# Weight conversion between attention and the first MLP: sign bit on GpSimd, value in PSUM, one piece every second period

## The chip, the cores and the metric

The kernel runs on one core of one Trainium2 chip. The metric is the device time of one execution in microseconds (us), lower is better. Engines are named as in the profile: PE is TensorE (PEld its weight loads), DVE is VectorE, ACT is ScalarE, POOL is GpSimd, SP is SyncE, whose queue starts nearly all of the DMA transfers.

## The reference

Attention over 4 batches, 8 heads, 576 positions and head dimension 64, with a learned bias that depends on relative position; then two MLPs on the 2304 tokens, each 512 to 2048 to 512:

```python
scores = scale * q @ k.T + bias            # bias = relu(x @ w1 + b1) @ w2, x from log1p of |i - j|
attn = softmax(scores);  x = attn @ v      # 2304 x 512 after the heads are put side by side
h = x @ w_in;   g = h - tanh(h);           x = g @ w_out       # first MLP
h = x @ w_in2;  r = max(h, 0); g = s*r*r + b;  out = g @ w_out2  # second MLP
```

The four weight matrices reach the kernel as 64-bit floats. The MLPs multiply in a split form: each operand becomes a rounded part ("high", fp32r) and the rest ("low"), and a product is three matmuls (high x high, high x low, low x high).

## The kernel before, in words

**Stages.** First the position bias is computed and written to DRAM. Then attention runs as 80 *periods*: 16 head pairs, `t` = 0 to 4 in each, two heads of 128 query rows per period (at `t` = 4, one tile of the two 64-row rests). Five periods are one pair. Then the MLPs run as 10 chunks of tokens (five of each layer; 512 tokens, one chunk of each layer 256), each with 16 *iterations* over the hidden blocks `f`.

**Order.** The order on every engine is the order in which the program is written (manual schedule); each engine works its own queue in that order and waits by semaphores. In iteration `n` of the attention loop the code emits: the normalisation of period n-2 (`emit_norm`, POOL, tile `pn`), the scores of period n (`emit_score`, PE, tile `s` in PSUM, two buffers), exp and row sum of n-1 (ACT; the sum `sm` gets an epsilon on POOL), bias and row minimum of n (`emit_bias`, DVE, L389, tiles `raw` and `mn`), the reciprocal of n-1 (DVE), transposes of n-3 (PE, L426) and their copies out of PSUM to `pt` (ACT and DVE), the products with V (PE, L481). At the end of the iteration come loads, pieces of the first chunk's input for the MLP (list `XPRE`: a load of `x`, its rounding "hi", L84, and rest "lo", L87, both on POOL), and weight conversion.

**Weight conversion.** A *half* is one 128 x 512 block of `w_in` or `w_out`; 32 halves make a layer. `wq` lists them in the order of use, `fetch` loads them. The two 32-bit words of each 64-bit number are turned into one fp32 value by integer arithmetic. One call of `weights_tick` is a pipeline of three halves:

- for half a: ACT scales the high word into tile `wx` (L138); DVE cuts out the sign bit into tile `wsg` (L139);
- for half a-1: DVE shifts the value and ors the sign in (L130), then ors in the top bits of the low word (L142);
- for half a-2: ACT rounds to the high part (L122), POOL subtracts to get the low part (L87).

In attention `TK` places 16 such calls (every fourth period from 15, then 66, 70, 74, 78). In the MLP loop, iteration n makes calls until `want` halves are done: 14 at the start, then 1.65 per iteration from n = 3; for the second layer's weights 1.4 per iteration from the fifth chunk on.

**MLP iteration.** `gemm1` (PE, 12 matmuls into the PSUM tile `h`, four buffers), `gate` (ACT reads `h` into `t`; DVE computes g into SBUF from `h` and `t`, in layer 2 from `t` alone and with a second instruction), then one iteration later `split` (ACT rounds g to `gh`, DVE subtracts to get `gl`), and two iterations later `gemm2` (12 matmuls into four PSUM accumulators).

Of the kernel before, what the change touches and what calls it, by code (L numbers as in the profile page):

```python
# [10 lines left out]
F32 = mybir.dt.float32  # L11
# [18 lines left out]
NW0 = 7  # L30

# [15 lines left out]
TK = [*range(15, 63, 4), 66, 70, 74, 78]  # L47
# [11 lines left out]
def tile_kernel(ctx, tc, qk, vd, wcat, wts, sb, ltab, psib, ipsi8, out):  # L59
# [26 lines left out]
    def rest(lo, raw, hi):  # L86
        nc.gpsimd.tensor_tensor(out=lo, in0=raw, in1=hi.bitcast(F32), op=ALU.subtract)  # L87
# [25 lines left out]

    def weights_tick():

        a, b_, c = wdone
        if c < b_:
            F, h = wq[c]
            x = wx_t.pop(c)[0]
            wdone[2] += 1  # L120
            w = wt[F, h] = slot(F, h, [2, 512], F32R)
            nc.scalar.copy(w[:, 0], x)  # L122
            rest(w[:, 1], x, w[:, 0])
        half = b_ < a
        if half:

            wdone[1] += 1
            x, sg = wx_t[b_]
            xi = x.bitcast(I32)
            nc.vector.scalar_tensor_tensor(out=xi, in0=xi, scalar=3, in1=sg,  # L130
                                           op0=ALU.logical_shift_left, op1=ALU.bitwise_or)
        if a < len(wq) and wq[a] in raw_w:

            wdone[0] += 1
            y = wst.tile([128, 512], F32, tag="wx", name="wx")
            sg = wsg.tile([128, 512], I32, tag="wsg", name="wsg")
            hw = raw_w[wq[a]][:, :, 1]
            nc.scalar.activation(out=y, in_=hw.bitcast(F32), func=AF.Copy, scale=2.0 ** -112)  # L138
            nc.vector.tensor_scalar(out=sg, in0=hw, scalar1=-2 ** 31, scalar2=1, op0=ALU.bitwise_and, op1=ALU.bitwise_or)  # L139
            wx_t[a] = (y, sg)  # L140
# [133 lines left out]
    def ring(dtype):  # L274
        return bp.tile([128, S], dtype, tag="bias", name="ring")
# [40 lines left out]
    def gate(c, f):  # L316
        layer, _, cn = CHUNKS[c]
        h = h_t.pop((c, f))
        g = ring(F32)[:, 0:cn]
        t = ring(F32)[:, 0:cn]  # L320
        if layer == 0:
            nc.scalar.activation(out=t, in_=h, func=AF.Tanh)  # L322
            nc.vector.tensor_tensor(out=g, in0=h, in1=t, op=ALU.subtract)  # L323
        else:
            nc.scalar.activation(out=t, in_=h, func=AF.Relu)  # L325
            nc.vector.tensor_tensor(out=g, in0=t, in1=t, op=ALU.mult)  # L326
            nc.vector.tensor_scalar(out=g, in0=g, scalar1=sb_t[:, 0:1], scalar2=sb_t[:, 1:2], op0=ALU.mult, op1=ALU.add)  # L327
        g_t[c, f] = (g, ring(F32R)[:, 0:cn], ring(F32R)[:, 0:cn])
# [7 lines left out]
    with ExitStack() as ca:  # L336
# [23 lines left out]
        TICKS = {n: TK.count(n) for n in TK}  # L360
# [140 lines left out]
        for n in range(NK + 6):  # L501
# [29 lines left out]
            for _ in range(TICKS.get(n, 0)):  # L531
                weights_tick()
# [7 lines left out]
    with ExitStack() as cb:  # L540
# [46 lines left out]
        xwork = {}  # L587
        seq = [(c, f) for c in range(len(CHUNKS)) for f in range(NF)]
# [4 lines left out]
        for n in range(len(seq) + LAG):  # L593
            want = min(32, 2 * NW0 + max(0, int(1.65 * (n - 3))))
# [85 lines left out]
```

## Time and profile before

| | |
|---|---|
| median of 3 runs | 1091.99 us (1091.46 to 1092.54) |
| the profiled execution: its own time, its span | 1091.09 us, 1089.3 us |
| PE busy | 1065.3 us (98%) |
| DVE busy | 642.6 us (59%) |
| ACT busy | 469.6 us (43%) |
| POOL busy | 327.5 us (30%) |
| attention, roughly | 48 to 303 us of the span |
| both MLPs | 303 to 1085 us of the span |

A matmul's end is modelled, so a busy PE need not be at its peak: what an engine waited for is read from idle time and its releaser, and from how far apart the same step of successive periods starts. PE's granted clock is at its upper level (2.4 GHz) in all but a few us of the span.

### The profile page before, as it was taken

To read this page: it belongs to the slowest core of one execution; us is meant where nothing else is said; L and a number is where in the kernel's file an instruction comes from. 1 tells how busy PE (TensorE), PEld (TensorE's weight loads), DVE (VectorE), ACT (ScalarE), POOL (GpSimd) and SP (SyncE) were. 2 spreads that over 40 slices of the span, in tenths; PEclk is the share of its full clock that TensorE was granted. 3 is DMA by queue.
4 is the path that set the end of the run, shared out by engine and by line. 5 is a ranking of instruction groups with operands and counts; after the bars stand their busy time and mean duration, and the time that the engine had idled before them with its cause. 6 is when DMAs were issued, how large, how long until landed. Compare 5 with 4: busy or idle time off the path is not lost.

```text
span 1089.3 us, 18185 instructions
## 1 busy us (share of the span) xinstructions
PE 1065.3 (98%) x7000; PEld 838.0 (77%) x7000; DVE 642.6 (59%) x1223; ACT 469.6 (43%) x955; POOL 327.5 (30%) x454
## 2 busy tenths in 40 slices
PE   9999999999999999999999999999999999999998
PEld 6566555555678888899888888888888888888897
DVE  8878889778679832232322499997343343343344
ACT  8977677677545422222222354553222222222222
POOL 0066777678625510020300046344030030010000
PEclk9999999999999999999999999999999999999999
DMA  7957555253181010020100365500100020010010
GB/s 283 314 191 257 189 180 183 85 180 113 42 318 65 10 59 1 0 79 1 58 1 1 135 218 206 193 1 20 58 20 1 4 75 1 1 58 1 1 39 20
DMA packets 41334, 99.65 MB, mean 91 GB/s; under 512 B 5024, under 2 KB 11552, under 8 KB 41248
## 3 DMA queue, kind: packets, MB, share of 16 engines
q1 hardware_dynamic: 40960, 98.24, 26.1%
q8 instruction: 55, 0.90, 0.3%
q10 hardware_dynamic: 288, 0.26, 0.1%
q14 instruction: 31, 0.25, 0.1%
HBM read 73.41 MB, written 25.07 MB: 90 GB/s over the span
## 4 chain that ended last, share of the span: by engine, by line
PE 83%; POOL 4%; DVE 3%; DMA 2%; issue 2%; ACT 1%; ACTq 0%; SPq 0%; DVEq 0%; POOLq 0%
PE h L312 36%; PE a L569 36%; PE o L481 5%; PE s L382 4%; POOL pn L420 3%; PE t L426 2%; DMA qk<-in_qk 1%; DVE raw L389 1%; POOL w L87 1%; DVE pt L464 1%; DMA vv<-in_vd 1%; PE c L426 0%; POOL sm L407 0%; DVE wx L142 0%; DVE wx L130 0%
## 5 line engine op out<-in xcount | busy, mean ns | idle before, releaser
L312 PE MATMUL h<-x,w 128*128 128x512 f32 (+1 forms) x1920 | 420.6, 368 | 0.0
L312 PEld LDWEIGHTS h<-x,w 128*128 128x128 f32 x1920 | 337.4, 188 | 62.4 <-issue 1.3
L569 PE MATMUL a<-ring,w 128*128 128x512 f32 (+1 forms) x960 | 210.2, 368 | 0.0
L569 PE MATMUL a<-w,ring 128*128 128x512 f32 x864 | 208.9, 389 | 0.0
L569 PEld LDWEIGHTS a<-ring,w 128*128 128x128 f32 x960 | 168.3, 189 | 30.0
L569 PEld LDWEIGHTS a<-w,ring 128*128 128x128 f32 x864 | 161.1, 188 | 32.8
L87 POOL TENSOR_TENSOR w<-wx,w 128x512 fp32r<-128x512 f32 x64 | 96.0, 1500 | 209.7 <-ACT w L122 196.4
L333 DVE TENSOR_TENSOR ring<-ring 128x512 fp32r<-128x512 f32 (+1 forms) x160 | 110.3, 690 | 78.5 <-ACT ring L332 78.5
L332 ACT CAST ring<-ring 128x512 fp32r<-128x512 f32 (+1 forms) x160 | 92.3, 577 | 135.7 <-DVE ring L327 96.6
L420 POOL TENSOR_SCALAR pn<-p,sm 128x576 f32<-128x576 f32 (+2 forms) x224 | 136.8, 627 | 36.1 <-DVE sm L411 30.5
L326 DVE TENSOR_TENSOR ring<-ring 128x512 f32<-128x512 f32 (+1 forms) x80 | 53.0, 662 | 149.9 <-ACT ring L325 149.9
L323 DVE TENSOR_TENSOR ring<-h,ring 128x512 f32<-128x512 f32 (+1 forms) x80 | 50.8, 635 | 141.0 <-ACT ring L322 140.7
L84 POOL TENSOR_SCALAR x<-xr 128x512 fp32r<-128x512 f32 (+1 forms) x36 | 25.9, 719 | 330.1 <-DMA xr<-x_d 330.1
L403 ACT ACTIVATE p<-raw,mn 128x576 f32<-128x576 f32 x144 | 110.7, 773 | 13.8 <-DVE mn L389 13.0
L325 ACT ACTIVATE ring<-h 128x512 f32<-128x512 f32 (+1 forms) x80 | 44.4, 555 | 165.7 <-PE h L312 165.7
L322 ACT ACTIVATE ring<-h 128x512 f32<-128x512 f32 (+1 forms) x80 | 44.3, 554 | 164.6 <-PE h L312 164.6
L389 DVE CUSTOM_DVE_ANT_0 raw<-s,bias 128x576 f32<-128x576 f32 x144 | 103.7, 752 | 18.5 <-PE s L382 14.6
L382 PE MATMUL s<-qk 64*128 64x288 f32 (+1 forms) x640 | 93.8, 433 | 11.5 <-DVE mn L389 11.1
L481 PE MATMUL o<-pt,vv 128*64 128x256 f32 (+1 forms) x640 | 96.0, 422 | 0.0
L382 PEld LDWEIGHTS s<-qk 64*128 64x128 f32 (+1 forms) x640 | 46.3, 175 | 55.7 <-DVE mn L389 24.4
L426 PEld LDWEIGHTS t<-ident,pn 64*128 64x128 f32 x1184 | 52.5, 140 | 16.8 <-DVE pt L464 6.0
L122 ACT CAST w<-wx 128x512 fp32r<-128x512 f32 x64 | 39.7, 621 | 58.8 <-DVE wx L142 57.7
(49 smaller groups left out, 841.0 us busy)
## 6 DMA issues: line engine op xcount, KB each, us to landing
w<-in_wts SPq DMA_DIRECT2D x64, 512.0 KB, 4.7
qk<-in_qk SPq DMA_DIRECT2D x16, 864.0 KB, 6.6
bias_d<-m SPq DMA_DIRECT2D x36, 296.0 KB, 4.4
bias<-bias_d SPq DMA_DIRECT2D x32, 288.0 KB, 4.7
xr<-x_d SPq DMA_DIRECT2D x28, 256.0 KB, 3.0
vv<-in_vd SPq DMA_DIRECT2D x16, 320.0 KB, 4.2
x_d<-o SPq DMA_DIRECT2D x16, 256.0 KB, 2.1
out_x<-o SPq DMA_DIRECT2D x16, 256.0 KB, 2.1
```

The lines of the kernel that those rows point to most:

```text
L87: nc.gpsimd.tensor_tensor(out=lo, in0=raw, in1=hi.bitcast(F32), op=ALU.subtract)
L312: nc.tensor.matmul(h, a, x, start=(k == 0), stop=(k == 3 * KD - 1))
L326: nc.vector.tensor_tensor(out=g, in0=t, in1=t, op=ALU.mult)
L332: nc.scalar.copy(gh, g)
L333: nc.vector.tensor_tensor(out=gl, in0=g, in1=gh.bitcast(F32), op=ALU.subtract)
L382: nc.tensor.matmul(o[0:n, c, 0:288], q[h, ee, t * 128:t * 128 + n], kk[h, ee], start=True, stop=True)
L389: nc.vector.tensor_tensor_reduce(out=raw.rearrange("p (c j) -> p c j", c=2), in0=s_t.pop((x, j))[:, :, 0:288], in1=bias_t[pairs[i][0], k]. ...
L403: nc.scalar.activation(out=p, in_=raw, func=AF.Exp, scale=-1.0, bias=mn, accum_out=sm[:, j:j + 1])
L420: nc.gpsimd.tensor_scalar(out=pn[:, c:c + b - a], in0=p[:, a:b], scalar1=sm[:, j:j + 1], scalar2=0.0, op0=ALU.mult, op1=ALU.add)
L426: nc.tensor.transpose(out_, in_, ident[ROWS[r], ROWS[r]])
L481: nc.tensor.matmul(o[h], v[:, e, j], unit_t[i, u][:, 8 if j == 4 else 4 * e + j, 0:n], start=(j == 0), stop=(j == 4))
L569: nc.tensor.matmul(o, x, y, start=first and j == 0, stop=last and j == 2)
```

## The change

Four things change together.

1. The sign comes from POOL: the high word, read as a float, times 0.0 gives a signed zero, whose bits are the sign bit. The DVE instruction L139 is gone; POOL has one more instruction per half.
2. The conversion is cut into four functions: `begin` (POOL sign, ACT value), `high` (DVE shift and or), `low` (DVE or of the low word), `both` (ACT rounding, POOL rest). In attention each is a piece of its own, at periods 15, 17, 19, ..., 77, so eight halves are done there (k = 0 to 7, four pieces each). `weights_tick` still exists for the MLP loop, with `high` and `low` next to each other.
3. In the MLPs the value lies in PSUM (pool `ps_y`, two buffers) between `begin` and `low`. Its two banks are taken from `h`, which has two buffers where it had four.
4. `gate` writes g over `h` in PSUM, in both layers; `split` reads it there. In layer 2 the square is h times relu(h) in place of relu(h) times itself.

The MLP loop begins with 8 halves done, makes one call in each of iterations 0 and 1, and then 1.9 halves per iteration from n = 2.

```diff
+RATE = 1.9
-TK = [*range(15, 63, 4), 66, 70, 74, 78]
+ND = 8
+TK = {15 + 2 * j: (j // 4, j % 4) for j in range(4 * ND)}
...
+    def begin(k):
+        raw = raw_w[wq[k]][:, :, 1].bitcast(F32)
+        if ypool:
+            y = ypool[0].tile([128, 512], F32, tag="y", name="y")
+        else:
+            y = wst.tile([128, 512], F32, tag="wx", name="wx")
+        sg = wsg.tile([128, 512], F32, tag="wsg", name="wsg")
+        nc.gpsimd.tensor_scalar(out=sg, in0=raw, scalar1=0.0, scalar2=1.0, op0=ALU.mult, op1=ALU.mult)
+        nc.scalar.activation(out=y, in_=raw, func=AF.Copy, scale=2.0 ** -112)
+        wx_t[k] = (y, sg)
+    def high(k):
+        y, sg = wx_t[k]
+        yi = y.bitcast(I32)
+        nc.vector.scalar_tensor_tensor(out=yi, in0=yi, scalar=3, in1=sg.bitcast(I32),
+                                       op0=ALU.logical_shift_left, op1=ALU.bitwise_or)
+    def low(k):
+        y = x = wx_t[k][0]
+        if ypool:
+            x = wst.tile([128, 512], F32, tag="wx", name="wx")
+        nc.vector.scalar_tensor_tensor(out=x.bitcast(I32), in0=raw_w.pop(wq[k])[:, :, 0], scalar=29, in1=y.bitcast(I32),
+                                       op0=ALU.logical_shift_right, op1=ALU.bitwise_or)
+        wx_t[k] = x
+    def both(k):
+        F, h = wq[k]
+        x = wx_t.pop(k)
+        w = wt[F, h] = slot(F, h, [2, 512], F32R)
+        nc.scalar.copy(w[:, 0], x)
+        rest(w[:, 1], x, w[:, 0])
...
     def gate(c, f):
-        g = ring(F32)[:, 0:cn]
         t = ring(F32)[:, 0:cn]
-        if layer == 0:
-            nc.scalar.activation(out=t, in_=h, func=AF.Tanh)
-            nc.vector.tensor_tensor(out=g, in0=h, in1=t, op=ALU.subtract)
-        else:
-            nc.scalar.activation(out=t, in_=h, func=AF.Relu)
-            nc.vector.tensor_tensor(out=g, in0=t, in1=t, op=ALU.mult)
-            nc.vector.tensor_scalar(out=g, in0=g, scalar1=sb_t[:, 0:1], scalar2=sb_t[:, 1:2], op0=ALU.mult, op1=ALU.add)
+        nc.scalar.activation(out=t, in_=h, func=(AF.Tanh, AF.Relu)[layer])
+        nc.vector.tensor_tensor(out=h, in0=h, in1=t, op=(ALU.subtract, ALU.mult)[layer])
+        if layer:
+            nc.vector.tensor_scalar(out=h, in0=h, scalar1=sb_t[:, 0:1], scalar2=sb_t[:, 1:2], op0=ALU.mult, op1=ALU.add)
...
-                hpool.append(h_ctx.enter_context(tc.tile_pool(name="ps_h", bufs=4, space=PSUM, side="right", reuse_waits="tile")))
+                for pool, name in ((hpool, "ps_h"), (ypool, "ps_y")):
+                    pool.append(h_ctx.enter_context(tc.tile_pool(name=name, bufs=2, space=PSUM, side="right", reuse_waits="tile")))
...
-            for _ in range(TICKS.get(n, 0)):
-                weights_tick()
+            if n in TK:
+                k, j = TK[n]
+                (begin, high, low, both)[j](k)
...
-            want = min(32, 2 * NW0 + max(0, int(1.65 * (n - 3))))
+            want = min(32, ND + max(0, int(RATE * (n - 2))))
+            if n < 2:
+                weights_tick()
```

How the change stands in the queues is shown at three places. First DVE, at period 47 of attention, before; the two `L389 ISA` rows are bias and minimum of one head, and L466 to L488 are copies out of PSUM:

```order
L411 RECIPROCAL sm<-sm 128x2
L466 COPY pt<-t_3342 128x4x64
L467 COPY pt<-t_3342 64x64
L488 COPY xo<-o 128x256
L130 SCALAR_TENSOR_TENSOR wx<-wx,wsg 128x512
L139 TENSOR_SCALAR wsg<-w_2028 128x512
L142 SCALAR_TENSOR_TENSOR wx<-w_2349,wx 128x512
L389 ISA raw,mn<-s,bias 128x576
L389 ISA mn 128x1
```

The same queue of the changed kernel at period 49, where the piece is `high` of half 4; period 47 (`begin`) and period 50 have no such instruction on DVE, and `low` stands in period 51:

```order
L480 COPY pt<-t_3415 128x8x64
L504 COPY xo<-o 128x320
L133 SCALAR_TENSOR_TENSOR wx<-wx,wsg 128x512
L405 ISA raw,mn<-s,bias 128x576
L405 ISA mn 128x1
L405 ISA raw,mn<-s,bias 128x576
```

Three conversion instructions in a row have become one, and the next period's bias stands behind one in place of three. Second POOL, at periods 59 to 61, before; `x_` is the MLP's first input, L420 the normalisation, L407 the row sum's epsilon:

```order
L407 TENSOR_SCALAR sm<-sm 128x2
L87 TENSOR_TENSOR w_4011<-wx,w_4011 128x512
L420 TENSOR_SCALAR pn<-p,sm 128x576
L420 TENSOR_SCALAR pn<-p,sm 128x512
L420 TENSOR_SCALAR pn<-p,sm 128x64
L407 TENSOR_SCALAR sm<-sm 128x1
L84 TENSOR_SCALAR x_4070<-ring 128x512
L420 TENSOR_SCALAR pn<-p,sm 128x576
L420 TENSOR_SCALAR pn<-p,sm 128x64
L407 TENSOR_SCALAR sm<-sm 128x2
L87 TENSOR_TENSOR x_4070<-ring,x_4070 128x512
L420 TENSOR_SCALAR pn<-p,sm 128x576
```

and of the changed kernel at periods 60 and 61:

```order
L423 TENSOR_SCALAR sm<-sm 128x1
L86 TENSOR_SCALAR x_4021<-ring 128x512
L436 TENSOR_SCALAR pn<-p,sm 128x576
L436 TENSOR_SCALAR pn<-p,sm 128x64
L423 TENSOR_SCALAR sm<-sm 128x2
L89 TENSOR_TENSOR x_4021<-ring,x_4021 128x512
L89 TENSOR_TENSOR w_4075<-wx,w_4075 128x512
L436 TENSOR_SCALAR pn<-p,sm 128x576
```

The weight's rest (L87 before, L89 now) has moved from period 59 to 61, right behind the rest of x. Third DVE at the start of the MLPs, changed kernel; L342 is `gate`, L350 `split`, L133 `high` and L140 `low`:

```order
L342 TENSOR_TENSOR h<-h,ring 128x512
L133 SCALAR_TENSOR_TENSOR y<-y,wsg 128x512
L140 SCALAR_TENSOR_TENSOR wx<-w_2338,y 128x512
L350 TENSOR_TENSOR ring<-h,ring 128x512
L133 SCALAR_TENSOR_TENSOR y<-y,wsg 128x512
L140 SCALAR_TENSOR_TENSOR wx<-w_2980,y 128x512
L342 TENSOR_TENSOR h<-h,ring 128x512
```

Every one of these four kinds has one operand in PSUM (`h` or `y`) and one in SBUF; before, only the first MLP's `gate` had.

## Rows read from the trace of the kernel before

**Rows 1.** Windows: first 62 us of the MLPs, and the sum to 1085.

```profile
core 0: us, PE busy (x) PEld busy (x) DVE busy (x) ACT busy (x) POOL busy (x), PEclk, DMA share, GB/s
303.00:365.00 62.00, 62.00 (x275) 51.35 (x274) 56.72 (x70) 31.29 (x55) 29.81 (x22) 1.00 0.45 173
...
sum 782.00, PE 782.00 PEld 658.99 DVE 394.02 ACT 244.20 POOL 149.10; mean PE 260.67 PEld 219.66 DVE 131.34 ACT 81.40 POOL 49.70
```

**Rows 2.** Chain of work that ended last, from 60 to 90 us.

```profile
by line: PE o L481 40.7%; PE s L382 39.4%; PE t L426 15.7%; PE c L426 4.5%
```

**Rows 3.** Timeline, PE: first scores of periods 6, 11, 15 and 75.

```profile
61.04 1.24 PE L382 MATMUL s<-qk 64*128 64x288 f32 x8
...
74.90 1.24 PE L382 MATMUL s<-qk 64*128 64x288 f32 x8
...
86.03 1.24 PE L382 MATMUL s<-qk 64*128 64x288 f32 x8
...
275.69 1.24 PE L382 MATMUL s<-qk 64*128 64x288 f32 x8
```

**Rows 4.** Groups by line, 89 to 303 us: weight conversion (busy, mean ns).

```profile
L87 POOL TENSOR_TENSOR w<-wx,w 128x512 fp32r<-128x512 f32 x13 | 18.2, 1403 | 15.3 <-ACT w L122 9.0 <-DVE pt L464 4.0 <-DVE pt L467 2.3
L130 DVE SCALAR_TENSOR_TENSOR wx<-wx,wsg 128x512 int32<-128x512 int32 x13 | 12.9, 989 | 0.0
L142 DVE SCALAR_TENSOR_TENSOR wx<-w,wx 128x512 int32<-128x512 int32 x13 | 12.6, 971 | 0.0
...
L139 DVE TENSOR_SCALAR wsg<-w 128x512 int32<-128x512 int32 x13 | 11.1, 856 | 0.0
```

**Rows 5.** Timeline around the call of period 47.

```profile
187.21 1.49 DVE L130 SCALAR_TENSOR_TENSOR wx<-wx,wsg 128x512 int32<-128x512 int32 x1
...
190.03 0.74 DVE L389 CUSTOM_DVE_ANT_0 raw<-s,bias 128x576 f32<-128x576 f32 x1
...
190.84 0.72 PE L382 MATMUL s<-qk 64*64 64x288 f32 x8 [1.73 <-DVE mn L389]
```

**Rows 6.** Timeline around the call of period 19.

```profile
100.06 0.79 PEld L382 LDWEIGHTS s<-qk 64*128 64x128 f32 x8 [0.67 <-DMA qk<-in_qk]
...
100.41 0.76 DVE L130 SCALAR_TENSOR_TENSOR wx<-wx,wsg 128x512 int32<-128x512 int32 x1
...
102.03 0.75 DVE L389 CUSTOM_DVE_ANT_0 raw<-s,bias 128x576 f32<-128x576 f32 x1
...
102.86 1.41 PE L382 MATMUL s<-qk 64*128 64x288 f32 x8
```

**Rows 7.** Timeline around the rest of x in period 65.

```profile
246.13 1.27 POOL L87 TENSOR_TENSOR x<-ring,x 128x512 fp32r<-128x512 f32 x1
...
246.73 1.24 PE L382 MATMUL s<-qk 64*128 64x288 f32 x8
...
249.53 1.24 PE L382 MATMUL s<-qk 64*128 64x288 f32 x8
```

**Rows 8.** Timeline around the rounding of x in period 60.

```profile
232.78 0.62 POOL L84 TENSOR_SCALAR x<-ring 128x512 fp32r<-128x512 f32 x1 [1.74 <-DMA ring<-x_d]
...
235.54 0.52 PE L426 MATMUL t<-ident,pn 64*128 64x64 f32 x9 [0.60 <-DVE pt L464]
...
238.91 0.68 PE L426 MATMUL t<-ident,pn 64*128 64x64 f32 x15 [0.92 <-DVE pt L467]
```

**Rows 9.** Timeline in the first MLP: DVE beside one POOL instruction.

```profile
341.48 1.61 POOL L87 TENSOR_TENSOR x<-xr,x 128x512 fp32r<-128x512 f32 x1
341.86 0.68 DVE L323 TENSOR_TENSOR ring<-h,ring 128x512 f32<-128x512 f32 x1
...
342.46 1.19 DVE L130 SCALAR_TENSOR_TENSOR wx<-wx,wsg 128x512 int32<-128x512 int32 x1
```

**Rows 10.** Timeline of two iterations in the first MLP without conversion.

```profile
405.99 0.69 DVE L333 TENSOR_TENSOR ring<-ring 128x512 fp32r<-128x512 f32 x1 [0.69 <-ACT ring L332]
...
406.50 2.88 PE L312 MATMUL h<-x,w 128*128 128x512 f32 x12
...
411.94 2.88 PE L312 MATMUL h<-x,w 128*128 128x512 f32 x12
```

More of the change, by code (lines that the diff above doesn't have):

```diff
@@ L112, in fetch @@
             raw_w[F, h] = raw.bitcast(I32).rearrange("p (n two) -> p n two", two=2)
+    ypool = []
+    def begin(k):
[8 more added lines that the diff above has]
+        wx_t[k] = (y, sg)
@@ L114, in weights_tick @@
+    def both(k):
[4 more added lines that the diff above has]
+        rest(w[:, 1], x, w[:, 0])
     def weights_tick():
         a, b_, c = wdone
+        fresh = a < len(wq) and wq[a] in raw_w
         if c < b_:
-            F, h = wq[c]
-            x = wx_t.pop(c)[0]
+            both(c)
             wdone[2] += 1
-            w = wt[F, h] = slot(F, h, [2, 512], F32R)
-            nc.scalar.copy(w[:, 0], x)
@@ L123, in weights_tick @@
-            rest(w[:, 1], x, w[:, 0])
-        half = b_ < a
-        if half:
-            wdone[1] += 1
[L128 to L132, printed above, removed]
-            wdone[0] += 1
[L135 to L140, printed above, removed]
@@ L141, in weights_tick @@
-        if half:
-            nc.vector.scalar_tensor_tensor(out=xi, in0=raw_w.pop(wq[b_])[:, :, 0], scalar=29, in1=xi,
-                                           op0=ALU.logical_shift_right, op1=ALU.bitwise_or)
+        if b_ < a:
+            high(b_)
+            low(b_)
+            wdone[1] += 1
+        if fresh:
+            begin(a)
+            wdone[0] += 1
     bp = ctx.enter_context(tc.tile_pool(name="bp", bufs=11))
@@ L318, in gate @@
         h = h_t.pop((c, f))
-        g = ring(F32)[:, 0:cn]
         t = ring(F32)[:, 0:cn]
-        if layer == 0:
-            nc.scalar.activation(out=t, in_=h, func=AF.Tanh)
-            nc.vector.tensor_tensor(out=g, in0=h, in1=t, op=ALU.subtract)
-        else:
-            nc.scalar.activation(out=t, in_=h, func=AF.Relu)
-            nc.vector.tensor_tensor(out=g, in0=t, in1=t, op=ALU.mult)
-            nc.vector.tensor_scalar(out=g, in0=g, scalar1=sb_t[:, 0:1], scalar2=sb_t[:, 1:2], op0=ALU.mult, op1=ALU.add)
-        g_t[c, f] = (g, ring(F32R)[:, 0:cn], ring(F32R)[:, 0:cn])
+        nc.scalar.activation(out=t, in_=h, func=(AF.Tanh, AF.Relu)[layer])
+        nc.vector.tensor_tensor(out=h, in0=h, in1=t, op=(ALU.subtract, ALU.mult)[layer])
+        if layer:
+            nc.vector.tensor_scalar(out=h, in0=h, scalar1=sb_t[:, 0:1], scalar2=sb_t[:, 1:2], op0=ALU.mult, op1=ALU.add)
+        g_t[c, f] = (h, ring(F32R)[:, 0:cn], ring(F32R)[:, 0:cn])
     def split(c, f):
@@ L359, in tile_kernel @@
             work.setdefault(5 * i - 3, []).append(lambda i=i: load_v(i))
-        TICKS = {n: TK.count(n) for n in TK}
         PRE = {}
@@ L587, in tile_kernel @@
         xwork = {}
+        wdone[:] = [ND] * 3
         seq = [(c, f) for c in range(len(CHUNKS)) for f in range(NF)]
```

## The prediction

> **What bounds the kernel now.** I read the windows by stage first, because the busy shares of the page are means over two very different stages. From 303 to 1085 us, both MLPs, PE is busy for 782.00 of 782.00 us, also in the first 62 us, where DVE is busy for 56.72 of 62.00 [rows 1]. No other engine's load can be seen in the end time there: the MLPs can be made slower by this change, but not faster.
>
> Then the chain of waits in a stretch of attention without weight conversion, 60 to 90 us: it consists of PE steps alone (40.7 + 39.4 + 15.7 + 4.5%, rounded, all of it) [rows 2]. So undisturbed attention is bound by PE too, and its pace is read from a score of one step to that of the next pair: 61.04 to 74.90, 13.86 us for five periods [rows 3]. Now the stretch in which weights are converted: the score of period 15 starts at 86.03, that of period 75 at 275.69, 189.66 us for twelve pairs [rows 3]. At PE's pace these would take 12 x 13.86 = 166.3 us. **The room is 23.3 us**, and it is all there is to win: whatever the change gives must come from these 60 periods.
>
> What fills the room is shown by one call of the weight conversion. After the call of period 47 DVE begins L130 at 187.21 and reaches the next bias only at 190.03; the score behind it waits 1.73 us for that bias [rows 5]. A call can also be free: after period 19, DVE is away from 100.41 to 102.03, and the next score but one starts at 102.86, 2.80 us after 100.06, with no PE wait shown on it [rows 6]. So 1.6 us away from the bias does not hurt and 2.8 us costs at least 1.7: a score has about one bias of lead, and a long run of DVE instructions exceeds it. Thirteen halves pass through this stage now, with 12.9 + 12.6 + 11.1 = 36.6 us of DVE time [rows 4].
>
> **The change part by part.**
>
> *Removed from attention.* Five halves of thirteen, and L139 for all: DVE's conversion time falls from 36.6 us to 8 x (0.99 + 0.97) = 15.7 us with today's means [rows 4]. More to the point, no run of three instructions is left. Taken alone this returns the whole room: -23.3 us.
>
> *Pieces on DVE.* Sixteen, `high` and `low`, each alone in its period with a free period behind it. Behind each stand the two biases of the next period, and the scores wait for those. Price of one: nothing at the lower end, as for the 1.62 us after period 19 [rows 6], since a piece has lasted 0.97 to 0.99 us on average [rows 4]. At the upper end the line from nothing through the long run, 1.73 us lost for 2.82 us away, or 0.61 us for a piece of 1 us [rows 5]. I take 0.1 us, close to the row of period 19, as a piece is shorter than that run: 1.6 us, between 0 and 9.8.
>
> *Pieces on POOL and ACT.* Eight `begin` and eight `both`. POOL's sign is a one-input instruction on 512 columns; the nearest row is the rounding of x with 0.62 us, the far one the two-input rest with 1.27 us, which reads as many operands as the strided word has halves [rows 7, 8]. I take 0.62. Behind each piece stand the next normalisation and the row sum, and DVE's reciprocal waits for that. The rest alone has cost nothing: one of 1.27 us starts at 246.13 and the scores follow each other by 2.80 us, the undisturbed step [rows 7]. At the upper end, POOL held for 1.74 + 0.62 + 1.27 us in periods 60 and 61 made PE wait 0.60 and 0.92 us [rows 7, 8], 0.42 us per us. So 1.9 us of POOL per half is between 0 and 0.8 us; I take 0.2, as each piece is no longer than the free one: 1.6 us for eight, between 0 and 6.4. The five rests that leave attention are in the room already.
>
> *The first chunk's input.* Its rounding stays where it was, and POOL will wait for the same load: the 1.5 us of PE waits [rows 8], of which I carry 2.0 us for this and its later pieces. New is that in period 61 the weight's rest stands right behind that of x, 1.27 us more in the worst place; I take half. 2.7 us, between 1.5 and 3.9.
>
> *Loads.* At PE's pace the q and k of the next pair are just in time: the weight load for period 20's score waits 0.67 us for them, and there the periods ahead had lost nothing [rows 6]. PE's weight loads run ahead of its matmuls, so I count a third of it, 0.2 us (an estimate). There are three such places, where biases and weights are loaded too. At the two later ones the periods ahead lose on average 23.3 / 16 = 1.5 us per call now; up to 1.2 us of that each can come back as a wait for the load, which is late next. 0.2 to 2.6 us, I take 1.4.
>
> *First MLP.* 24 halves in place of 19 have to pass here, at 1.9 per iteration. An iteration is 5.44 us of PE (406.50 to 411.94) [rows 10]. DVE: two instructions of `gate` and `split` at 0.69 [rows 10] and 3.8 pieces at 0.68, the length of an instruction with one operand in PSUM [rows 9]: 4.0 us. POOL: 1.9 x (1.27 + 0.62) = 3.6 us, and 7.6 us for a chunk's input over some seven iterations, 4.7. Both are under 5.44, while DVE now runs at 56.72 of 62.00 [rows 1]. The first weight not yet ready is used in iteration 5, three iterations after the loop's first gemm1, so there is lead as well. Two buffers of `h`: gemm1 of n+2 needs `split` of n. In an iteration without conversion that ends at 406.68, 2.7 us after a gemm1 that started 5.44 us before 406.50, and the gemm1 two later starts at 411.94 [rows 10]: 5.3 us to spare, more than the two pairs of pieces (2.7 us) that can stand ahead of it. Cost nothing; the cover is PE's own 5.44 us, and without it each us that DVE or POOL exceeds it is lost once per iteration.
>
> *A rule against the pieces.* Under a POOL instruction of 1.61 us a DVE instruction with one operand in PSUM took 0.68 us, and the next, with both in SBUF, 1.19 us, ending 0.56 us after POOL's [rows 9]; L139 and the other two have means of 0.86 to 0.99 us in attention [rows 4]. In attention the pieces keep both operands in SBUF, and `high` or `low` comes just when POOL normalises. The Trainium skill (SBUF — State Buffer, section Who interferes with whom) says that such a DVE instruction and a GpSimd instruction that reads SBUF exclude each other for a whole instruction, in the order of their start; the trace agrees. By that rule a piece would last 1.5 us as L130 did beside POOL [rows 5], which is still under 1.62 us, and would hold POOL up in turn; that result is the first rival.
>
> **Sum.** -23.3 + 1.6 + 1.6 + 2.7 + 1.4 = **-16.0 us**. From the profiled execution's 1091.1 us that is 1075.1; the median of the runs is 0.9 us above that execution, so I say **1076.0 us**.
>
> **Rivals.**
>
> 1. *The pieces interfere with POOL.* Each DVE piece takes 1.5 us, delays the normalisation, and both effects reach PE: 0.61 x 1.5 = 0.9 us for half of the sixteen and 0.8 us for half of the eight halves' POOL work, 10.6 us in place of 3.2. Time 1083.4. For it: L130's 1.49 us [rows 5]. Against it: 1.62 us were free once [rows 6].
> 2. *Everything is hidden.* Pieces cost nothing, loads arrive: 1.7 us remain, 1070.4. For it: rows 6 and 7 show each kind of piece free. Against it: they were single cases, at one step of a pair each.
> 3. *It ends slower: the conversion in the first MLP is late.* If the pieces with PSUM operands took long, or POOL's sign did, `both` would come after the gemm1 that needs it. DVE exceeds 5.44 us when a piece lasts more than (5.44 - 1.38) / 3.8 = 1.07 us. At 1.5 us an iteration would take 7.1, 1.6 us too much, times 12.6 iterations: 20 us, all of the gain, 1096. It decides from about 1.4 us on. For it: DVE is nearly full there today [rows 1], and no row shows DVE writing to PSUM. Against it: a read of PSUM cost it nothing [rows 9].
> 4. *No change.* The waits move from DVE to the loads one for one, within 0.2% (some 2.2 us, about what a measurement of this kernel can tell): 1092. Only the three places with a load just in time speak for it.
>
> **How the numbers follow.** Forecast (gain of 13 to 20 us) 0.58; rival 1 (4 to 13 us) 0.21; rival 2 (over 20 us) 0.12; rival 3 0.06, of which 0.04 ends slower by over 0.2%; rival 4 0.03. The range takes the forecast and reaches into rivals 1 and 2: **1071 to 1086 us**. Faster 0.93, same 0.03, slower 0.04.
>
> **What would show it.** In the changed kernel's profile: scores of period 15 and 75 some 173 to 174 us apart; PE's waits on the minimum `mn` few and short; pieces L133 and L140 at 0.7 to 1.5 us in attention and near 0.7 us in the MLPs; POOL's sign (L126) near 0.62 us; the largest remaining waits at the x rounding of periods 60 to 63 and at the q and k loads; PE busy without a gap from 303 us (then some 16 us earlier) on. The prediction is wrong if scores still wait over 1 us behind single pieces, if gemm1 waits for a weight or for `h`, or if the loads set the pace of the pairs.

## The result, and the profile after

The changed kernel takes 1078.28 us (median of 4 runs, 1076.36 to 1080.47); the kernel before, run beside it, 1091.84 us (4 runs, 1091.46 to 1092.54). The ratio is 0.9876, with a 95% interval of 0.9856 to 0.9896: 13.6 us faster, where 16.0 were forecast, and inside the predicted range. The profiled execution took 1078.75 us with a span of 1077.0, so it is 12.3 us shorter than that of before.

The windows of the changed kernel come first, over the first 60 us and over nearly all of the rest of the MLPs. Columns: the stretch, its length, then busy us and instruction count of PE, PEld, DVE, ACT and POOL, the granted clock, the DMA share and GB/s.

```profile
290.00:350.00 60.00, 60.00 (x267) 49.26 (x264) 41.34 (x64) 34.80 (x64) 41.75 (x44) 1.00 0.47 178
350.00:1070.00 720.00, 720.00 (x3447) 607.70 (x3446) 302.76 (x463) 206.58 (x382) 125.78 (x139) 1.00 0.14 47
```

PE is as full as it was [rows 1]. DVE, busy for 56.72 of 62.00 us before, now has 41.34 of 60.00. The first gemm1 starts at 279.05 us and the span ends 797.95 us later:

```profile
279.05 0.73 PE L333 MATMUL h<-x,w 128*128 128x512 f32 x2
```

Before, it started at 291.33 us, and 797.97 us were left:

```profile
291.33 0.73 PE L312 MATMUL h<-x,w 128*128 128x512 f32 x2
```

So the MLPs kept their length, and the gain lies wholly ahead of 279 us.

There the score of period 15 and that of period 75 are read again (start, duration, engine, line, tiles, shapes):

```profile
86.82 1.24 PE L398 MATMUL s<-qk 64*128 64x288 f32 x8
...
262.00 1.24 PE L398 MATMUL s<-qk 64*128 64x288 f32 x8
```

They are 175.18 us apart where they were 189.66 [rows 3]: the twelve pairs gained 14.5 us and are still 8.9 above PE's 166.3. PE's waits from 80 to 290 us are listed below: what waited for what, us in total, how often, the longest.

```profile
PE t L442 <- DVE pt L483: 2.8, 2, 1.8
PE t L442 <- DVE pt L480: 1.6, 3, 0.7
PE s L398 <- DMA qk<-in_qk: 0.9, 1, 0.9
```

In the same stretch of the kernel before, scores waited ten times for `mn`, 10.1 us in all:

```profile
PE s L382 <- DVE mn L389: 10.1, 10, 1.7
```

That line is gone. What is left are transposes (L442) that wait until `pt` is copied out of PSUM, and one load.

The 8.9 us are not spread over the pairs. From the starts of the scores, three pairs lose 1.1 to 1.2 us each (in periods 19, 23 and 39), one loses 4.3 (the pair that starts with period 60), the others 0.4 or less. The loss of period 19 is the load: the next score, at 101.80 us, waits for q and k. Two periods ahead of 23 and 39, at the end of 21 and 37, stands the piece `both`; the normalisation queued behind it is the one that the transposes of 23 and 39 need. Here are POOL and the engines around it on the way to period 23, from the timeline (the bracket is the idle time before, and what ended it):

```profile
106.98 0.62 ACT L148 CAST w<-wx 128x512 fp32r<-128x512 f32 x1
...
107.68 1.28 POOL L89 TENSOR_TENSOR w<-wx,w 128x512 fp32r<-128x512 f32 x1 [1.46 <-DVE pt L480]
...
110.95 0.17 DVE L427 RECIPROCAL sm<-sm 128x2 f32<-128x2 f32 x1 [1.30 <-POOL sm L423]
...
111.83 0.68 PE L442 MATMUL t<-ident,pn 64*128 64x64 f32 x15 [0.95 <-DVE pt L483]
```

POOL's rest (L89) needs ACT's rounding (L148), and that ends only at 107.60. The view names DVE's copy as releaser, but the rest starts 0.08 us after ACT's end. POOL stands idle for 1.46 us, with the next normalisation and row sum queued behind the rest. DVE then waits 1.30 us for the sum, copies `pt` late, and PE waits 0.95 us.

In periods 60 to 63 the same chain is longer, since x's load is late too:

```profile
219.73 0.62 POOL L86 TENSOR_SCALAR x<-ring 128x512 fp32r<-128x512 f32 x1 [2.30 <-DMA ring<-x_d]
...
221.72 1.27 POOL L89 TENSOR_TENSOR x<-ring,x 128x512 fp32r<-128x512 f32 x1
...
222.95 1.28 POOL L89 TENSOR_TENSOR w<-wx,w 128x512 fp32r<-128x512 f32 x1
...
226.22 0.17 DVE L427 RECIPROCAL sm<-sm 128x2 f32<-128x2 f32 x1 [2.44 <-POOL sm L423]
...
227.10 0.68 PE L442 MATMUL t<-ident,pn 64*128 64x64 f32 x15 [1.81 <-DVE pt L483]
```

POOL loses 2.30 us on the load and then does the two rests one behind the other; the transpose waits 1.81 us. The two windows around it (columns as above) show a second loss: after a stretch in which PE was busy for 1.47 of 3.40 us, the granted clock is 0.52, that is 1.2 GHz nearly throughout, for the next 3.40 us.

```profile
224.40:227.80 3.40, 1.47 (x23) 0.84 (x22) 1.53 (x5) 1.75 (x5) 2.67 (x6) 1.00 0.01 2
227.80:231.20 3.40, 3.40 (x18) 1.06 (x20) 1.73 (x7) 2.66 (x6) 3.23 (x7) 0.52 0.45 128
```

Last, the conversion's instructions in attention (86 to 290 us; count, then busy us and mean ns of one, then idle time before them):

```profile
L89 POOL TENSOR_TENSOR w<-wx,w 128x512 fp32r<-128x512 f32 x8 | 10.2, 1279 | 6.5 <-ACT w L148 2.8 <-DVE pt L483 2.3 <-DVE pt L480 1.5
L133 DVE SCALAR_TENSOR_TENSOR wx<-wx,wsg 128x512 int32<-128x512 int32 x8 | 7.0, 873 | 0.0
L140 DVE SCALAR_TENSOR_TENSOR wx<-w,wx 128x512 int32<-128x512 int32 x8 | 6.9, 866 | 0.0
L126 POOL TENSOR_SCALAR wsg<-w 128x512 f32<-128x512 f32 x10 | 6.6, 665 | 0.6
```

and in the first MLP (290 to 370 us), where one operand lies in PSUM:

```profile
L89 POOL TENSOR_TENSOR w<-wx,w 128x512 fp32r<-128x512 f32 x24 | 31.1, 1296 | 29.2 <-ACT w L148 28.5 <-DMA w<-in_wts 0.7
L133 DVE SCALAR_TENSOR_TENSOR y<-y,wsg 128x512 int32<-128x512 int32 x24 | 16.6, 691 | 1.1 <-POOL wsg L126 1.1
L140 DVE SCALAR_TENSOR_TENSOR wx<-w,y 128x512 int32<-128x512 int32 x24 | 16.5, 688 | 0.8
L126 POOL TENSOR_SCALAR wsg<-w 128x512 f32<-128x512 f32 x22 | 14.3, 648 | 0.0
```

The 6.5 us of idle time on the eight rests of attention are the finding: POOL waits there. Not each of these waits reaches PE: the rest of period 45 waits longest, 1.60 us, and its pair loses 0.2 us. In the MLP, with the pieces at 0.69 us, nothing is late.

### The profile page after: what moved, and what is told of

It reads as the page before. It is cut to its first block, busy times and chain, and to the rows that moved or that the text cites. A ratio compares the mean times of both kernels' runs of the same rounds, so it can differ in the third digit from the quotient of the medians.

```text
span 1077.0 us, 18296 instructions
## 1 busy us (share of the span) xinstructions
PE 1062.1 (99%) x7000; PEld 837.2 (78%) x7000; DVE 572.8 (53%) x1159; ACT 461.9 (43%) x955; POOL 340.5 (32%) x518
## 4 chain that ended last, share of the span: by engine, by line
PE 90%; POOL 2%; DVE 1%; issue 1%; DMA 1%; ACT 1%; SPq 0%; ACTq 0%; DVEq 0%; POOLq 0%
PE h L333 37%; PE a L587 36%; PE o L497 7%; PE s L398 6%; PE t L442 3%; POOL pn L436 1%; PE c L442 1%; DMA qk<-in_qk 1%; POOL w L89 0%; DVE pt L480 0%; ACT p L419 0%; DVE raw L405 0%; POOL sm L423 0%; SPq L113 0%; DVE pt L483 0%
## 5 line engine op out<-in xcount | busy, mean ns | idle before, releaser
L342 DVE TENSOR_TENSOR h<-h,ring 128x512 f32<-128x512 f32 (+1 forms) x160 | 103.4, 646 | 348.1 <-ACT ring L341 347.9
L349 ACT CAST ring<-h 128x512 fp32r<-128x512 f32 (+1 forms) x160 | 87.1, 544 | 142.8 <-DVE h L344 108.0
L436 POOL TENSOR_SCALAR pn<-p,sm 128x576 f32<-128x576 f32 (+2 forms) x224 | 133.1, 610 | 36.5 <-DVE sm L427 36.5
L350 DVE TENSOR_TENSOR ring<-h,ring 128x512 fp32r<-128x512 f32 (+1 forms) x160 | 101.8, 636 | 74.2 <-ACT ring L349 69.3
L86 POOL TENSOR_SCALAR x<-xr 128x512 fp32r<-128x512 f32 (+1 forms) x36 | 20.6, 572 | 339.2 <-DMA xr<-x_d 338.0
L89 POOL TENSOR_TENSOR w<-wx,w 128x512 fp32r<-128x512 f32 x64 | 82.8, 1294 | 88.6 <-ACT w L148 84.2
L126 POOL TENSOR_SCALAR wsg<-w 128x512 f32<-128x512 f32 x64 | 41.8, 653 | 83.5 <-DMA w<-in_wts 82.9
L442 PEld LDWEIGHTS t<-ident,pn 64*128 64x128 f32 x1184 | 52.8, 139 | 15.2 <-DVE pt L480 4.0
L344 DVE TENSOR_SCALAR h<-h,sb_t 128x512 f32<-128x512 f32 (+1 forms) x80 | 61.2, 766 | 2.9
L442 PE MATMUL t<-ident,pn 64*128 64x64 f32 x1184 | 56.5, 224 | 5.8 <-DVE pt L480 2.9
```

The lines of the kernel that those rows point to most:

```text
L342: nc.vector.tensor_tensor(out=h, in0=h, in1=t, op=(ALU.subtract, ALU.mult)[layer])
L349: nc.scalar.copy(gh, g)
L350: nc.vector.tensor_tensor(out=gl, in0=g, in1=gh.bitcast(F32), op=ALU.subtract)
L436: nc.gpsimd.tensor_scalar(out=pn[:, c:c + b - a], in0=p[:, a:b], scalar1=sm[:, j:j + 1], scalar2=0.0, op0=ALU.mult, op1=ALU.add)
L442: nc.tensor.transpose(out_, in_, ident[ROWS[r], ROWS[r]])
```

## The experiments

The theory: the gain comes from the long DVE runs, of which none is left; what remains of the room is the waiting `both`, x's load, and the q and k loads. The rivals: the pieces' own length, the sign's new engine, or fewer halves as such. "Pairs" below is the time from the score of period 15 to that of 75, against 166.3 at PE's pace. The runs came in three groups, each with its own runs of the kernel before: 1092.1 us for the first four, 1092.36 for the next four, 1093.4 for the last two.

**e0_again.** The changed kernel as it is (one unused constant added).

> The changed kernel once more, to see how far its runs lie apart and where. Its runs were 1076.4 to 1080.5 us. If the difference between runs sits in the waits of periods 60 to 64 (a late load of x, and a stretch at the lower clock after the wait), the profile shows a loss of 2 to 5 us there and the twelve pairs from period 15 take 173 to 176 us; if it sits elsewhere, these pairs agree within 0.5 us with the 175.2 us of the first profile.

Measured: 1077.3 us, ratio 0.9866 [0.9852, 0.9879], pairs 175.38. The losses stand in the same periods, and the 1.2 GHz stretch is there too. The start differs: the score of period 15 begins at 85.82 us here, at 86.82 in the first profile, and at 85.8 to 87.6 over all profiles of kernels that do not differ up to there. The 0.8 us later start of the first profile is thus no effect of the change.

**e1_rest_later.** ACT's rounding stays, POOL's rest comes one period later.

```diff
-    def both(k):
+    def cast(k):
...
-        nc.scalar.copy(w[:, 0], x)
-        rest(w[:, 1], x, w[:, 0])
+        nc.scalar.copy(w[:, 0], wx_t[k])
+    def remain(k):
+        w = wt[wq[k]]
+        rest(w[:, 1], wx_t.pop(k), w[:, 0])
...
-                (begin, high, low, both)[j](k)
+                (begin, high, low, cast)[j](k)
+            if n - 1 in TK and TK[n - 1][1] == 3:
+                remain(TK[n - 1][0])
```

> Only the POOL half of the piece `both` moves, one period later, so that ACT's rounding is done when POOL comes to it. Theory: what is left of the room is mostly POOL's, which stands 1.1 to 1.5 us idle before L89 with the normalisation queued behind; then the losses at periods 23 and 39 (1.2 us each) go, and part of the 4.2 us at 63 and 64: 1074 to 1076.5 us against 1078.3. Rival, the loads of q and k set what is left: the waits return as waits for loads, within 0.5 us of 1078.3. Rival, the DVE pieces cost: no change either, and the scores wait for `mn`.

Measured: 1073.94 us, 0.9834 [0.9821, 0.9846], 3.4 us less than e0_again, pairs 171.07. The timeline of POOL near period 23 now shows a rest without a wait:

```profile
109.56 1.27 POOL L89 TENSOR_TENSOR w<-wx,w 128x512 fp32r<-128x512 f32 x1
```

and PE's waits from 80 to 290 us are (its lines shift by 6):

```profile
PE t L448 <- DVE pt L486: 1.4, 3, 0.9
PE s L404 <- DMA qk<-in_qk: 1.3, 1, 1.3
PE t L448 <- DVE pt L489: 0.8, 1, 0.8
```

Periods 23 and 39 are back at the undisturbed 2.89 and 3.18 us. Period 63 takes 3.95 us where it took 6.23, and the clock stays at 2.4 GHz. The pair of period 20 still loses 0.3 us, now in period 24. The same work in the same engines' queues, one step later, costs little: it was the wait, not the length of a single piece.

**e2_x_later.** Rounding and rest of the first part of x one period later, `both` as in the change.

```diff
-XPRE = [(-22, "load", 0), (-20, "hi", 0), (-19, "lo", 0), (-18, "load", 1), (-16, "hi", 1), (-15, "lo", 1),
+XPRE = [(-22, "load", 0), (-19, "hi", 0), (-18, "lo", 0), (-18, "load", 1), (-16, "hi", 1), (-15, "lo", 1),
```

> Only the rounding and the rest of the first block of x move, by one period, from 60 and 61 to 61 and 62. Theory: POOL no longer waits 2.3 us for the load of x, and the weight's rest in period 61 no longer stands behind that of x: of the 4.2 us lost in this pair 2 to 3.5 go, 1075 to 1076.5 us. Rival, the POOL work itself (0.62 + 1.27 + 1.28 us in two periods) is too much wherever it stands: less than 1 us, 1077.5 or more.

Measured: 1075.6 us, 0.9852 [0.9839, 0.9865], pairs 172.27. The interval overlaps that of e0_again; the trace is clearer: the pair of period 60 takes 15.68 us in place of 18.04, and all other pairs are unchanged but for 0.8 us of the load wait.

**e3_bursts.** Eight halves in attention, as in the change, but as whole calls every sixth period: rest, `high`, `low` and sign of different halves at once.

```diff
-TK = {15 + 2 * j: (j // 4, j % 4) for j in range(4 * ND)}
+TK = {15 + 6 * j: j for j in range(ND + 2)}
...
-                k, j = TK[n]
-                (begin, high, low, both)[j](k)
+                k = TK[n]
+                if k >= 2:
+                    both(k - 2)
+                if 1 <= k <= ND:
+                    high(k - 1)
+                    low(k - 1)
+                if k < ND:
+                    begin(k)
```

> The same 8 halves with the same instructions in attention (sign from POOL), but as calls of the old pipeline every sixth period: `both` of k-2, `high` and `low` of k-1 next to each other, `begin` of k. Theory: a DVE run of 1.4 to 1.9 us is about what one bias of lead covers (1.6 us were free), so little is lost on DVE, and POOL's rest and sign in one period cost about what `both` costs now: 1079 to 1084 us. Rival, it is the spreading into single pieces that gave the gain: each of eight runs costs 1.5 to 1.9 us as a call did before, 1088 to 1092 us.

Measured: 1086.14 us (6 runs, 1082.39 to 1087.66), 0.9948 [0.9934, 0.9962]; pairs 180.87 in the profiled execution, which was the shortest. It lies between the two expectations: against e0_again, by the medians, the cut into pieces is worth 8.8 us, and the rest of the change the other 6.0. The profiled executions differ by 4.4 us only (1082.39 and 1077.95); the longer runs of e3_bursts show a mean granted clock of 0.995 to 0.998 where the profiled one has 1.000, so part of the 8.8 us may be clock; no trace shows where. The waits of PE show the old line again:

```profile
PE s L398 <- DVE mn L405: 4.8, 6, 1.4
PE t L442 <- DVE pt L480: 3.9, 6, 1.2
PE t L442 <- DVE pt L483: 1.2, 1, 1.2
```

It isn't a test of the run's length alone. POOL's rest and sign of the same call run beside `high` and `low`, and from 86 to 290 us these last 1152 and 1213 ns on average, 2.4 us a run, where single pieces last 873 and 866; POOL's sign lasts 930 ns in place of 665.

**e4_sign_dve.** In attention alone the sign goes back to DVE, beside ACT's value in `begin`.

```diff
-        nc.gpsimd.tensor_scalar(out=sg, in0=raw, scalar1=0.0, scalar2=1.0, op0=ALU.mult, op1=ALU.mult)
+        if ypool:
+            nc.gpsimd.tensor_scalar(out=sg, in0=raw, scalar1=0.0, scalar2=1.0, op0=ALU.mult, op1=ALU.mult)
+        else:
+            nc.vector.tensor_scalar(out=sg.bitcast(I32), in0=raw.bitcast(I32), scalar1=-2 ** 31, scalar2=1,
+                                    op0=ALU.bitwise_and, op1=ALU.bitwise_or)
```

> The changed kernel, but in attention the sign comes from DVE again (the old instruction, as part of the piece `begin`, alone in its period); the MLPs as changed. Theory: DVE has room for single instructions, so where the sign is made does not matter in attention: 1076.5 to 1079 us against 1077.3 for the changed kernel in the last job. Rival, taking the sign off DVE is what gave the gain there: eight more DVE instructions of 0.4 to 1.5 us reach PE, 1081 us or more.

Measured: 1077.15 us, 0.9861 [0.9842, 0.9879], pairs 174.57. No difference from e0_again that can be told, to about 2 us: eight single DVE pieces of 654 ns, in place of eight on POOL, change no period but those of the load and of x by more than 0.1 us, and the sign's engine gives nothing in attention.

**e6_value_sbuf.** In the first MLP the value stays in SBUF and `h` has its four buffers; the sign stays on POOL.

```diff
-        if ypool:
-            y = ypool[0].tile([128, 512], F32, tag="y", name="y")
-        else:
+        if True:
             y = wst.tile([128, 512], F32, tag="wx", name="wx")
...
-        if ypool:
-            x = wst.tile([128, 512], F32, tag="wx", name="wx")
...
-                for pool, name in ((hpool, "ps_h"), (ypool, "ps_y")):
-                    pool.append(h_ctx.enter_context(tc.tile_pool(name=name, bufs=2, space=PSUM, side="right", reuse_waits="tile")))
+                hpool.append(h_ctx.enter_context(tc.tile_pool(name="ps_h", bufs=4, space=PSUM, side="right", reuse_waits="tile")))
```

> The changed kernel, but in the MLPs the value stays in SBUF (and h has four buffers again); the sign still comes from POOL. Theory: PSUM only keeps DVE and POOL out of each other's way in the MLPs. DVE then needs about 1.9 x (0.98 + 0.83) + 1.4 = 4.8 us per iteration of 5.44 and POOL waits in between: PE has few waits, 1077 to 1081 us. Rival, without PSUM the conversion in the first MLP is late: more than 5 us of PE waits on weights between 290 and 360 us, 1083 us or more.

Measured: 1083.11 us, 0.9913 [0.9893, 0.9933], 6.0 above e4_sign_dve of the same group. The theory's 1077 to 1081 missed and its rival's number held. The groups of the conversion from 290 to 370 us:

```profile
L136 DVE SCALAR_TENSOR_TENSOR wx<-w,wx 128x512 int32<-128x512 int32 x24 | 35.7, 1487 | 0.8
L89 POOL TENSOR_TENSOR w<-wx,w 128x512 fp32r<-128x512 f32 x22 | 33.4, 1520 | 24.2 <-ACT w L144 24.2
L131 DVE SCALAR_TENSOR_TENSOR wx<-wx,wsg 128x512 int32<-128x512 int32 x24 | 23.6, 982 | 3.0 <-POOL wsg L124 3.0
L124 POOL TENSOR_SCALAR wsg<-w 128x512 f32<-128x512 f32 x22 | 22.8, 1035 | 0.0
```

and PE's waits from 285 to 400 us:

```profile
PE h L329 <- POOL w L89: 4.4, 2, 2.2
```

All four kinds of instruction are 17 to 116% longer than with the value in PSUM, on DVE and on POOL alike, and gemm1 waits for the low part of a weight. From the first gemm1 to the end the span is 803.7 us long in place of 797.95, so the loss stands in the MLPs.

**e9_old_in_mlp.** As e6_value_sbuf, and the sign in the MLPs on DVE as well: attention of the change, MLP conversion of before at the new rate.

```diff
+        if hpool:
+            nc.vector.tensor_scalar(out=sg.bitcast(I32), in0=raw.bitcast(I32), scalar1=-2 ** 31, scalar2=1,
+                                    op0=ALU.bitwise_and, op1=ALU.bitwise_or)
+        else:
+            nc.gpsimd.tensor_scalar(out=sg, in0=raw, scalar1=0.0, scalar2=1.0, op0=ALU.mult, op1=ALU.mult)
```

> Pieces and eight halves in attention as changed, but the MLPs convert in the old way: sign on DVE, value in SBUF, at 1.9 halves per iteration. Theory: DVE would need 1.9 x (0.98 + 1.06 + 0.83) + 1.5 = 6.9 us per iteration of 5.44; the 24 halves take 12.6 iterations, which makes 18 us too much, less what eight halves of lead and the slack to the use cover (6 to 10 us): PE waits 8 to 12 us on weights or on `gate`, 1085 to 1090 us. So the sign on POOL and PSUM pay by letting attention give up five halves. Rival, they pay nothing: 1077 to 1079 us.

Measured: 1086.83 us (5 runs), 0.9955 [0.994, 0.997], 9.7 above e4_sign_dve. The MLPs take 807.2 us. DVE is busy for 57.00 of the 60.00 us from 290 to 350, PE for 56.76, and PE's waits from 285 to 400 us are:

```profile
PE h L333 <- POOL w L89: 5.2, 6, 1.1
PE h L333 <- ACT w L148: 0.7, 2, 0.4
```

These are 5.9 of the 9.3 us by which the MLPs got longer; weight loads of PE wait for the same parts. Against e6_value_sbuf, the sign on POOL is worth 3.7 of the 9.7 us.

**e7_q_earlier.** e1_rest_later, and q and k of a pair loaded one period earlier.

```diff
-            work.setdefault(5 * i - 4, []).append(lambda i=i: load_qk(i))
+            work.setdefault(5 * i - 5, []).append(lambda i=i: load_qk(i))
```

> The kernel with POOL's rest one period later (1073.9 us), and q and k of each pair are asked for one period earlier, ahead of a weight's load and of four bias loads. Theory of the loads: the wait of period 20's score (1.3 us) goes, and nothing else: 1072 to 1073 us. Rival: the transfers share the same DMA engines, so the biases come later and make DVE wait instead: 1073.5 to 1075 us.

Measured: 1071.87 us (1071.1 to 1072.87), 0.9816 [0.9801, 0.983], pairs 168.58, only 2.3 us above PE's pace. This is the fastest version, 5.3 us ahead of e4_sign_dve in the same group, with intervals apart. All of PE's waits from 80 to 290 us:

```profile
PE t L448 <- DVE pt L486: 1.3, 3, 0.9
```

and POOL's rounding of x:

```profile
214.24 0.62 POOL L86 TENSOR_SCALAR x<-ring 128x512 fp32r<-128x512 f32 x1 [0.44 <-DMA ring<-x_d]
```

The wait for q and k is gone, and also most of that for x, 0.44 us where it was 1.87 in e1_rest_later and 2.30 in the changed kernel. That was not what the edit aimed at. Between 205 and 222 us x's loads take 4.2 us from issue to landing where one took 5.9 in e1_rest_later and 6.2 in the changed kernel, and the 864 KB of q and k are issued a period earlier, further ahead of them; that this is the reason was not tried by itself. Period 63 takes 2.89 us.

**e10_twelve.** e7_q_earlier with twelve halves in attention, in single pieces at three of four periods.

```diff
-ND = 8
-TK = {15 + 2 * j: (j // 4, j % 4) for j in range(4 * ND)}
+ND = 12
+TK = {15 + 4 * j // 3: (j // 4, j % 4) for j in range(4 * ND)}
```

> The fastest kernel so far (rest one period later, q and k asked for earlier, 1071.9 us) with twelve halves in attention as single pieces, three in every four periods, in place of eight. It asks whether the number of halves or the single pieces gave the gain. Theory: with pieces in neighbouring periods DVE and POOL get no free period to catch up; DVE is then busy for 11.3 + 2.2 of 13.9 us per pair, POOL for 9 + 2.0, so little is left, but single pieces still do not make runs: 1073 to 1078 us. Rival, the number of halves decides: four halves more cost four times what a call cost (1.5 to 1.8 us), 1078 us or more.

Measured: 1076.93 us, 0.9849 [0.9832, 0.9866], pairs 173.46. Against e7_q_earlier the pairs grew by 4.9 us for 16 more pieces, 0.3 each; PE's waits on `pt` grew from 1.3 us to:

```profile
PE t L448 <- DVE pt L486: 3.2, 6, 0.9
PE t L448 <- DVE pt L489: 1.5, 2, 0.7
```

The run changes more than the number of pieces and their spacing, though: at eight places the rest of one half and the sign of another now come in the same period. Here is POOL behind period 36, one instruction straight behind the other, and the normalisation (L442) late behind both:

```profile
148.42 0.67 POOL L126 TENSOR_SCALAR wsg<-w 128x512 f32<-128x512 f32 x1
149.05 1.28 POOL L89 TENSOR_TENSOR w<-wx,w 128x512 fp32r<-128x512 f32 x1
150.30 1.72 POOL L442 TENSOR_SCALAR pn<-p,sm 128x576 f32<-128x576 f32 x3
```

Two periods later, in period 38, a transpose waits 0.74 us and 1.0 us is lost. Periods 43, 54 and 59 lose 0.8 to 1.0 us in the same way, two periods behind 41, 52 and 57. These four make 3.7 of the 4.9 us. So POOL's doubled pieces are the larger part of the price; twelve halves with sign and rest kept apart weren't tried, and what density alone costs stays open.

**e11_pairs.** e7_q_earlier with `high` and `low` of a half together in `low`'s period.

```diff
-                (begin, high, low, cast)[j](k)
+                if j == 2:
+                    high(k)
+                if j != 1:
+                    (begin, high, low, cast)[j](k)
```

> The same fastest kernel with eight halves, but `high` and `low` next to each other in one period (the period of `low`), nothing else moved. It asks for the price of a DVE run of 1.4 to 1.9 us by itself; in the run with calls every sixth period POOL's and ACT's parts stood in the same period. Theory from the row of period 19, where 1.6 us away cost nothing: 1072 to 1074 us. Rival, the run is what exceeds the score's lead: 0.6 to 1.3 us lost for each of eight, 1077 to 1082 us.

Measured: 1074.78 us, 0.9832 [0.9817, 0.9846], pairs 172.16. It is between the two expectations. The ratio's interval overlaps that of e7_q_earlier a little; in the traces the pairs grew by 3.6 us, 0.45 for each run of two, and scores wait for `mn` once more:

```profile
PE t L448 <- DVE pt L486: 1.9, 4, 0.9
PE s L404 <- DVE mn L411: 1.7, 3, 0.7
```

The loss isn't even: the pairs of periods 25, 50 and 65 grow by 1.0 to 1.1 us each (the runs behind periods 27, 51 and 67), that of period 60 by 0.5, the others by 0.2 at most. The run behind period 19 is free.

With the cut pieces the loss goes with the step `t` of the pair. Runs of two on DVE cost 1.0 to 1.1 us at `t` = 1 and 2 (periods 51, 27, 67) and 0.5 or less elsewhere. A sign and a rest together on POOL (e10_twelve) cost 0.8 to 1.0 us at `t` = 1 and 2 (36, 41, 52, 57) and about 0.5 at most elsewhere (20, 25, 68, 73). The waiting rests of the changed kernel cost 1.1 us or more at `t` = 1 and 2 (21, 37, 61) and 0.2 at most elsewhere (29, 45, 53, 69). Whole calls cost at other steps too (e3_bursts, 1.5 us behind period 33, `t` = 3). Why these two steps have the least lead was not tried.

## Why the prediction was right, step by step

**Where the time is.** Right. All of the gain lies in periods 15 to 75 (14.5 us of the 23.3 of room), and the MLPs' 797.97 us became 797.95.

**Long DVE runs as the cause.** Right in the main: no score waits for `mn` in the changed kernel; runs of two with nothing else moved (e11_pairs) bring that wait back, 1.7 us of it and 3.6 us in the pairs; whole calls (e3_bursts) bring 4.8 us of it back, with the POOL and ACT parts of a call beside the run. That about one bias of lead, some 1.6 us, is the measure everywhere is not borne out: the step at which a run stands counts as much. The call of period 19 [rows 6], from which the text argued that 1.6 us away is free, was at a favourable step, `t` = 4: two pieces in one period, about 1.7 us by the lengths above, are free there in e11_pairs too, and cost 1.0 to 1.1 us at three other places.

**DVE pieces, 1.6 us.** Measured: little. They were 0.87 us long, and the eight pairs without another cause lose 1.1 us together, which is the most that the pieces in them, POOL's too, can have cost. Eight more (e4_sign_dve) changed nothing that shows. Rival 1, pieces of 1.5 us that reach PE, did not come: such lengths were seen only where POOL's rest and sign ran beside the pieces, 1.15 and 1.21 us on average in e3_bursts, 0.98 and 1.49 in e6_value_sbuf.

**POOL and ACT pieces, 1.6 us.** Periods 23 and 39 alone lost 2.3 us. The step that failed is "each piece is no longer than the free one": for a single piece, length was not the point. The free rest of x [rows 7] had its rounding a period ahead; the weight's rest follows its own rounding at once, across engines, and blocks POOL's queue meanwhile. e1_rest_later shows it, since the order alone removes all but 0.3 us of the loss. Two pieces in a row do hold POOL too long, without any wait, at some steps (e10_twelve).

**x, 2.7 us.** Measured 4.3 in the pair of period 60, just over the upper bound of 3.9. The collision of the two rests was foreseen, and e1_rest_later and e2_x_later, which separate them by one period in either way, leave 1.7 and 1.8 us. With x's load early too (e7_q_earlier) 0.5 us is left. What was left out of the sum is the 1.2 GHz stretch behind the 1.81 us wait: 0.48 of 3.40 us of PE, an estimate of some 1.6 us. Two figures of this term don't follow from the rows named: 2.0 us is carried from waits of 1.5 us, and 2.0 + 1.27 would make the upper bound 3.3, not 3.9.

**Loads, 1.4 us.** 1.1 us measured, all in one place (the score of period 20), and gone in the trace of e7_q_earlier; the two later places lost nothing to loads.

**First MLP, nothing.** Right, and rival 3 is answered: pieces that write and read PSUM took 0.69 us, under its 1.07. The two buffers of `h` cost nothing, as no gemm1 waits in the changed kernel; g over `h` in PSUM was in every run but the kernel before, so it was not tried by itself. Without PSUM for the value (e6_value_sbuf) DVE's pair takes 0.98 + 1.49 us, the weights are late and 6.0 us go. The Trainium skill (SBUF — State Buffer, section Who interferes with whom) says that a DVE instruction with both inputs in SBUF and a GpSimd instruction that reads SBUF exclude each other; the runs agree, 0.98 and 1.49 us with SBUF and 0.69 with one operand in PSUM, at the same work on POOL.

**The balance.** Pairs: 1.13 (load) + 2.33 (`both`) + 4.28 (x) + 1.14 (the rest) = 8.9 us of the room lost, against 7.3 in the sum. Beyond it the stretch from period 75 to the first gemm1 grew from 15.64 to 17.05 us, 1.4 that the sum had not; a transpose waits 0.73 us for `pt` there. It is the weight pieces at the end of attention: in e3_bursts, whose last one stands in period 69, the stretch takes 15.64 us without a wait, with x's last part in 78 and 79 as here. POOL stands idle for 1.13 us before the rest of period 77, as before that of period 37, so `both` is the likely one; with its rest in 78, behind the rounding of x, the stretch still takes 16.77 us (e1_rest_later). The 0.8 us of the later start come and go by themselves. The forecast is thus nearer than its terms were: DVE's pieces cost less than they were put at, x and the end of attention more.

So the change is one thing with two halves. The single pieces, and fewer halves, give the time in attention; the sign on POOL gives none there and the value lies in PSUM in the MLPs only, but the two let the first MLP take the five halves that attention gives up: at that rate the old conversion costs 9.7 us (e9_old_in_mlp) of the gain.

## What to carry to other kernels

Where a saturated engine has about one small instruction of lead, cut the side work into single instructions, no two of them on one engine in the same step, and look in the trace which steps bear one: here the same two instructions cost about 1 us at two steps of five and half of that or less at the others. An instruction whose operand another engine makes in the same step should be queued a step later: while it waits, everything behind it on its engine waits as well, and that, more than its length, was the price here. Before moving side work into a stage, see whether the two engines that do it read the same memory at once; one operand in PSUM was enough to keep DVE and POOL apart here.

## What the runs showed of the hardware that was not expected

- A wait of 1.81 us on PE was followed by 3.40 us at a granted clock of 0.52 (1.2 GHz nearly throughout) in an otherwise full stretch. It stands at this place in all five kernels with this wait, e0_again and e4_sign_dve among them; with a wait of 0.82 us there (e1_rest_later) or 0.96 us (e2_x_later) the clock stayed at 1.00. The kernel before has such a stretch too, 0.51 from 191.8 to 195.2 us, behind the 1.73 us wait of [rows 5]; but behind its other wait of 1.73 us, which ends at 127.64 us, the clock stayed at 1.00 from 126.8 to 133.6 us. So a wait of this length goes with the fall, and doesn't bring it each time.
- DVE's scalar_tensor_tensor in place in PSUM, with the other operand in SBUF, took 691 ns, and from PSUM to SBUF 688 ns: the write to PSUM cost nothing more. The one-input TENSOR_SCALAR of layer 2 did get longer in PSUM, from 629 to 819 ns (64 of them), without any effect on the time.
- When DVE and POOL block each other, a one-input POOL instruction suffers too: the sign took 1035 ns in e6_value_sbuf and 648 in the changed kernel's first MLP.
